# Routed rows kept as two 16-bit parts from PSUM on, transposed by DMA, and two tiles routed at once

## The chip, the cores and the metric

The kernel runs on one core of a Trainium2 chip. The metric is the device time of one execution in microseconds (us). Engines are named as in the profile: PE (TensorE matmul) and PEld (its weight loads), DVE (VectorE), ACT (ScalarE), POOL (GpSimd) and SP (SyncE, which issues nearly all DMAs here, in the order of its program).

## The reference

Local attention with ALiBi-like biases, then a dense layer of three maxed products, then a routed layer of eight experts, each token in its best one:

```python
x = attention(q, k, v)                                  # 3072 tokens x 512
h = np.maximum(np.maximum(x @ w1, x @ w2), x @ w3)      # 512 -> 768
x = h @ w_out                                           # 768 -> 512
logits = x @ w_gate
e_idx = np.argmax(logits, axis=1)
gate_w = softmax(logits)[np.arange(N), e_idx]
eom = 1.0 / (1.0 + np.exp(-(x @ w_output_gate)))
for e in range(8):
    mask = e_idx == e
    ye = np.maximum(x[mask] @ w1[e], 0.0) @ w2[e]       # 512 -> 1024 -> 512
    out[mask] = gate_w[mask, None] * eom[mask, e, None] * ye
```

All inputs are float32, and products are made from two 16-bit parts of each operand (high times high, high times low, low times high).

## The kernel before

The 3072 tokens are 24 tiles of 128 rows. Most of the program is written out by a planner: `Plan.run` picks from open tasks (generators that yield `op`, `dma`, `take` and `need`) the operation that by its own costs can start first, and so fixes the order on every engine. Engines then run their own list in order and wait at semaphores.

- **Attention** (tiles u = 0 to 23: `a_T`, `a_v`, `a_scores`, `a_trans`, `a_out`). `a_trans` transposes 512 KB of 16-bit weights by a DMA from SP (L1001).
- **Dense layer** in chunks of two tiles (`m_load`, `m_1`, `m_max`, `m_2`), woven into the attention from chunk 0 on. PE work of `m_1` is L1134, that of `m_2` is L1191.
- **Routing**, one task `m_route` per tile. `m_2` copies the second product out of PSUM as float32 rows `x2`. `split_T` transposes them on PE (L1065, four 128x128 float32 transposes), ACT copies the high part out and DVE makes the low part (`x2s`). Eight gate matmuls (L1225), a matmul that sums parts and turns the result (L1237), some 18 small DVE operations, two matmuls that count places (L1256, L1257), and POOL scatters the rows to `xs` in DRAM by expert (L1294).
- **First expert** (`pro_load`, `pro_1`, `pro_next`): the expert with most of the first 16 tiles' tokens is run on 256 rows while the last tiles are routed and `lists` works out the steps of the loop.
- **Expert loop** (`step`, 13 steps of two tiles here; `own` 0 and 1 are its two experts). PE order in a step: first product of own 0 (L1673, 96 matmuls), four float32 transposes of the next rows (`x_T`, L1595), first product of own 1, four transposes, second product of own 0, second product of own 1 (L1627). ACT and DVE split the transposed rows (L1597, L200). `load` fetches the rows for the step after that (L1586), and `split` takes the weights of the next expert, 8 pieces of 512 KB, from float32 to two parts and has each buffer loaded again (L1565).

L195 and L200 are the lines of the helpers `sub` and `low_of`, which many steps share.

Of the kernel before, what the change touches and what calls it, by code (L numbers as in the profile page):

```python
# [67 lines left out]
class Plan:  # L68
# [310 lines left out]
def local_attention_moe_kernel(  # L379
# [41 lines left out]
    make_identity(nc, ident)  # L421

# [131 lines left out]
    def buf(tag):  # L554
# [20 lines left out]
    wgp = cp.tile([P, KD, 4 * E], F32R, name="wgp")  # L575

    x_t = [mo.tile([P, D], F32, name=f"x{n}") for n in range(2)]
    x2_all = mo.tile([P, -(-3 * XW // LINE) * LINE], F32, name="x2r")
    x2_t = [x2_all[:, n * XW : (n + 1) * XW] for n in range(3)]
    stock("x", x_t)  # L580
    stock("x2s", [[mo.tile([P, KD, P], F32R, name=f"x2s{n}") for n in range(2)]])
# [8 lines left out]
                lg=mo.tile([4 * E, P], F32, name=f"lg{n}"),  # L590
                pz=mo.tile([P, 2 * E], F32, name=f"pz{n}"),
                rt=mo.tile([P, 5, E], F32, name=f"rt{n}"),
                rs=mo.tile([P, 6], F32, name=f"rs{n}"),
                ob=mo.tile([P, E], BF16, name=f"ob{n}"),
                di=mo.tile([P, 1], I32, name=f"di{n}"),
                one=mo.tile([P, 1], F32, name=f"one{n}"),
            )
            for n in range(2)
# [70 lines left out]
    def route_constants():  # L669
# [389 lines left out]
    def split_T(src, x, dst, s):  # L1059

        bank = yield take("bank")
        pt = bank.t.rearrange("p (a b) -> p a b", b=P)
        for d in range(KD):
            yield op(PE, 0.109, [src], [bank])
            nc.tensor.transpose(pt[:, d, :], x[:, d * P : (d + 1) * P], ident)  # L1065
        h, l = dst.t[0][:, :, s], dst.t[1][:, :, s]
        yield op(ACT, act(D), [bank], [dst])
        nc.scalar.copy(out=h, in_=pt)
        yield psum(dve(D), [bank, dst], [dst])
        sub(nc.vector, l, pt, h.bitcast(F32))  # L1070
        give("bank", bank)

# [105 lines left out]
    def m_2(c, t):  # L1178
# [29 lines left out]
        yield op(DVE, 0.2, [x2], [])  # L1208
        at = A_L + NTILE + tile_
        nc.vector.tensor_reduce(out=chk[:, at : at + 1], in_=x2.t[:, :NLOW], axis=AX.X, op=ALU.max)  # L1210
        plan.add(m_route(tile_, x2), (0, tile_))


    def m_route(tile_, x2):
        yield need(("wg",))
        xs_ = yield take("x2s")
        state("x2s", tile_)
        yield from split_T(x2, x2.t, xs_, slice(0, P))
        bank = yield take("bank")

        pl = bank.t[: 4 * E, :P]
        for n, d in [(4 * E, 0), *((2 * E, d) for d in range(KD)), *((4 * E, d) for d in range(1, KD))]:
            yield op(PE, 0.06, [xs_], [bank])
            X = xs_.t[0 if n == 4 * E else 1]
            nc.tensor.matmul(  # L1225
                pl[:n], lhsT=wgp[:, d, :n], rhs=X[:, d, :], start=(n, d) == (4 * E, 0), stop=(n, d) == (4 * E, KD - 1)
            )
# [3 lines left out]
        yield op(ACT, 0.25, [bank], [rb])  # L1231
        nc.scalar.copy(out=R["lg"], in_=pl)
        give("bank", bank)
        bank = yield take("bank")
        pz_ = bank.t[:, : 2 * E]
        yield op(PE, 0.19, [rb], [bank])
        nc.tensor.matmul(pz_, lhsT=R["lg"], rhs=two, start=True, stop=True)  # L1237
        pz, rt, rs, ob, di = R["pz"], R["rt"], R["rs"], R["ob"], R["di"]
        lz, tm, oh, ex, tz = [rt[:, n] for n in range(5)]
        mx, km, se, zs, co, de = [rs[:, n : n + 1] for n in range(6)]  # L1240
        yield psum(0.166, [bank], [rb])
        nc.vector.tensor_reduce(out=mx, in_=pz_[:, :E], axis=AX.X, op=ALU.max)

        yield psum(0.226, [bank, rb], [rb])
        nc.vector.scalar_tensor_tensor(out=tm, in0=pz_[:, :E], scalar=mx, in1=rev, op0=ALU.is_ge, op1=ALU.mult)
        yield op(DVE, 0.16, [rb], [rb])
        nc.vector.tensor_reduce(out=km, in_=tm, axis=AX.X, op=ALU.max)
        yield op(DVE, 0.18, [rb], [rb])
        nc.vector.tensor_scalar(out=ob, in0=rev, scalar1=km, scalar2=None, op0=ALU.is_equal)
        yield psum(0.18, [bank], [rb])  # L1250
        nc.vector.tensor_copy(out=pz, in_=pz_)
        give("bank", bank)
        bank = yield take("bank")
        pr = bank.t[:, : 2 * E].rearrange("p (a b) -> p a b", a=2)
        yield op(PE, 0.02, [rb], [bank])
        nc.tensor.matmul(pr[:, 0, :], lhsT=tri, rhs=ob, start=True, stop=True)  # L1256
        nc.tensor.matmul(pr[:, 1, :], lhsT=ones, rhs=ob, start=True, stop=True)  # L1257
        yield op(DVE, 0.16, [rb], [rb])
        nc.vector.tensor_scalar(out=lz, in0=pz[:, :E], scalar1=mx, scalar2=None, op0=ALU.subtract)
        yield op(DVE, 0.18, [], [])  # L1260
        nc.vector.tensor_scalar(out=oh, in0=rev, scalar1=km, scalar2=None, op0=ALU.is_equal)
        yield op(ACT, 0.4, [], [])
        nc.scalar.activation(out=ex, in_=lz, func=AF.Exp, accum_out=se)
        yield op(DVE, 0.16, [], [])
        nc.vector.tensor_mul(out=tz, in0=oh, in1=pz[:, E:])
        yield op(DVE, 0.16, [], [rb])
        nc.vector.tensor_reduce(out=zs, in_=tz, axis=AX.X, op=ALU.add)
        if tile_:
            yield need(("cnt", tile_ - 1), *([("snap",)] if tile_ == NFIRST else []))
        yield psum(0.16, [bank], [])  # L1270
        nc.vector.tensor_add(out=tm, in0=cnt, in1=pr[:, 0, :])
        yield op(DVE, 0.16, [], [])
        nc.vector.tensor_add(out=cnt, in0=cnt, in1=pr[:, 1, :])
        give("bank", bank)
        state("cnt", tile_)
        if tile_ == NFIRST - 1:
# [4 lines left out]
        nc.vector.tensor_tensor_reduce(out=tm, in0=tm, in1=oh, scale=1.0, scalar=0.0, op0=ALU.mult, op1=ALU.add, accum_out=de)  # L1281
        yield op(DVE, 0.16, [], [])
        nc.vector.tensor_copy(out=di, in_=de)
        yield op(ACT, 0.2, [rb], [rb])
        nc.scalar.activation(out=zs, in_=zs, func=AF.Exp, scale=-1.0)
# [4 lines left out]
        yield op(DVE, 0.16, [], [x2, rb])  # L1290
        nc.vector.reciprocal(out=x2.t[:, D + 1 :], in_=co)  # L1291
        yield op(POOL, 1.1, [x2, rb], [], 2.0, port=False)
        nc.gpsimd.memset(R["one"], 1.0)
        i = nc.gpsimd.indirect_dma_start(  # L1294
            out=xs[:, :], out_offset=bass.IndirectOffsetOnAxis(ap=di[:, 0:1], axis=0), in_=x2.t[:, :], in_offset=None
        )
        apart(i, "every token has a row of its own")
        give("x2r", x2)
        give("rt", rb)
        state("routed", tile_)  # L1300
# [270 lines left out]
    def fresh():  # L1571
# [3 lines left out]
        for name in ("pTx", "pg00", "pg01", "pg10", "pg11", "pc", "pd"):  # L1575
            T[name] = Buf(None, True)
# [11 lines left out]
    def x_T(half, step=False):  # L1588

        xr, xb = G["xr"][half], T[f"xT{half}"]  # L1590
        pTx = G["pTx"].rearrange("p (a b) -> p a b", b=P)
        xh, xl = [t[:, :, half * P : (half + 1) * P] for t in G["xE"]]
        for d in range(KD):
# [4 lines left out]
        yield psum(dve(D) + 0.07, [T["pTx"], xb], [xb])  # L1598
        low_of(nc, xl, pTx, XS, xh, G["sums"][:, NPC + half : NPC + half + 1] if step else G["acc"][:, NS + 6 + half : NS + 7 + half])
# [56 lines left out]
    def step(then, pl):  # L1656
# [5 lines left out]
        for own in range(2):  # L1662
            W, Wb = G["W"][1 - own], T["W"][1 - own]
            xT = [t[:, :, own * P : (own + 1) * P] for t in G["xE"]]
            for half in range(2):
# [11 lines left out]
                at = NPC + 2 + 2 * own + half  # L1677
# [6 lines left out]
            yield from x_T(own, True)  # L1684
# [12 lines left out]
    def pro_load():  # L1697
# [13 lines left out]
        G["xE"] = xT.t  # L1711
        for t, xb in enumerate(xbs):
            bank = yield take("bank")
            pt = bank.t.rearrange("p (a b) -> p a b", b=P)
            for d in range(KD):
                yield op(PE, 0.109, [xb], [bank])
                nc.tensor.transpose(pt[:, d, :], xb.t[:, d * P : (d + 1) * P], ident)
# [215 lines left out]
```

## Time and profile before

| | |
|---|---|
| time, median of 3 runs (lowest, highest) | 921.12 us (920.97, 921.45) |
| the profiled execution: time, span | 920.74 us, 919.2 us |
| PE busy | 851.1 us (93% of the span) |
| DVE, ACT, POOL busy | 689.0, 498.8, 225.2 us |
| DMA queue of SP, share of 16 engines' time | 56.2% |

The span is the stretch that the trace covers; the 1.5 us beside it lie before and after. The attention's last output is at about 471 us, the dense layer's last product ends at 592 us, and the loop runs from 617 to about 902 us. Busy time of PE counts each matmul until its modelled end, and neighbours overlap, so what an instruction costs on PE is read from the distance between starts.

### The profile page before, as it was taken

What the parts mean: (1) busy time and instruction counts of PE and PEld (TensorE: products, weight loads), DVE (VectorE), ACT (ScalarE), POOL (GpSimd) and SP (SyncE); (2) the same over time, 40 slices, a digit from 0 to 9 for tenths busy, and PEclk for the clock granted to TensorE, in tenths of its full rate; (3) what the DMA queues carried; (4) which work ended last, traced back from release to release, by engine and by line L of the source; (5) the groups of instructions that cost most, each with busy time, mean ns of one, the idle gap of its engine ahead of it and who ended that gap; (6) DMA issues with size and microseconds to landing.
All of it is one profiled execution on the core that took longest, in us unless ns stands there. A gap on an engine that the chain in (4) does not pass through costs nothing. (4 is left out here: it accounts for less than half of the span.)

```text
span 919.2 us, 24473 instructions
## 1 busy us (share of the span) xinstructions
PE 851.1 (93%) x8737; PEld 662.6 (72%) x8737; DVE 689.0 (75%) x2163; ACT 498.8 (54%) x1095; POOL 225.2 (24%) x245
## 2 busy tenths in 40 slices
PE   3566999899999999999999999999999999999993
PEld 2456876787878787878787787767777777777771
DVE  5998877888887877887767743367777777777774
ACT  4777766666666657576526322215555555555552
POOL 3444432223122213212101001012222222222222
PEclk9978999999999999999999999999999999999997
DMA  6997467777757776684558000047777766766600
GB/s 197 263 248 208 98 130 136 156 159 178 158 128 168 177 150 133 153 194 105 128 161 310 14 24 24 2 147 267 253 242 233 246 235 220 238 227 217 217 23 26
DMA packets 218907, 151.51 MB, mean 165 GB/s; under 512 B 181025, under 2 KB 181025, under 8 KB 218821
## 3 DMA queue, kind: packets, MB, share of 16 engines
q1 hardware_dynamic: 214658, 137.79, 56.2%
q0 software_dynamic: 4160, 12.62, 3.6%
q8 instruction: 48, 0.79, 0.4%
q14 instruction: 39, 0.31, 0.1%
q10 hardware_dynamic: 2, 0.00, 0.0%
HBM read 118.56 MB, written 23.11 MB: 154 GB/s over the span
## 5 line engine op out<-in xcount | busy, mean ns | idle before, releaser
L1134 PE MATMUL bank<-xT,w 128*128 128x256 f16 x2592 | 306.2, 275 | 2.7 <-ACT xT L1101 1.4
L1134 PEld LDWEIGHTS <-w 128*128 128x128 f16 x2592 | 249.3, 99 | 40.6 <-issue 6.6
L1673 PEld LDWEIGHTS <-we 128*128 128x128 f16 x2496 | 141.6, 98 | 4.6 <-ACTq L1877 0.8
L1673 PE MATMUL bank<-xT,we 128*128 128x128 f16 x2496 | 144.0, 219 | 0.9 <-DVEq L1877 0.6
L1627 PEld LDWEIGHTS <-he 128*128 128x128 f16 x672 | 65.7, 98 | 75.7
L981 ACT ACTIVATE sp<-sp,mn 128x232 f32<-128x232 f32 (+1 forms) x192 | 90.1, 470 | 45.1 <-DVE mn L974 43.9
L1616 ACT ACTIVATE hm<-bank 128x512 f32<-128x512 f32 x56 | 33.5, 597 | 136.8 <-issue 92.0
L1191 PE MATMUL bank<-w,hh 128*128 128x512 f16 x432 | 102.4, 379 | 0.0
L1156 DVE SCALAR_TENSOR_TENSOR hm<-bank,hm 128x512 f32<-128x512 f32 x72 | 49.7, 690 | 54.9 <-PE bank L1134 51.9
L1294 POOL DMA_INDIRECT xs<-x2r,di x24 | 24.6, 1026 | 238.3 <-DVE x2r L1291 99.8
L1627 PE MATMUL bank<-we,he 128*128 128x512 f16 x360 | 80.3, 379 | 0.0
L1627 PE MATMUL bank<-wp,he 128*128 128x512 f16 x312 | 69.5, 379 | 0.0
L1191 PEld LDWEIGHTS <-hh 128*128 128x128 f16 x432 | 40.7, 98 | 39.2 <-DVE hh L195 0.5
L200 DVE SCALAR_TENSOR_TENSOR wp<-ws,wp 128x1024 f16<-128x1024 f32 x56 | 66.2, 1217 | 0.0
L851 POOL TENSOR_SCALAR qkn<-qkn,vs 128x512 f32<-128x512 f32 x23 | 39.0, 1696 | 102.6 <-DVE vs L846 57.4
L974 DVE CUSTOM_DVE_ANT_0 sp<-bank,bias 128x232 f32<-128x232 f32 x160 | 60.1, 388 | 2.6 <-PE bank L950 2.5
L195 POOL TENSOR_TENSOR seen<-x,dco 128x1 f32<-128x1 f32 x14 | 13.2, 940 | 193.4 <-DVE x L1632 193.4
L200 DVE SCALAR_TENSOR_TENSOR we<-ws,we 128x1024 f16<-128x1024 f32 x49 | 59.7, 1220 | 0.0
L950 PE MATMUL bank<-k,qh 64*128 64x232 f32 (+1 forms) x384 | 44.0, 318 | 16.7 <-ACT k L924 12.0
L200 DVE SCALAR_TENSOR_TENSOR he<-hm,he 128x512 f16<-128x512 f32 x56 | 38.8, 692 | 20.2 <-ACT he L1620 17.0
L195 DVE TENSOR_TENSOR nat<-sp,nat 128x928 f16<-128x928 f32 (+1 forms) x46 | 52.7, 1146 | 1.3 <-ACT nat L995 0.3
L1549 ACT ACTIVATE wp<-ws 128x1024 f16<-128x1024 f32 x55 | 53.4, 1044 | 0.0
(264 smaller groups left out, 1402.4 us busy)
## 6 DMA issues: line engine op xcount, KB each, us to landing
ws<-in_moe_w_dram SPq DMA_DIRECT2D x112, 512.0 KB
raw<-in_moe_w_dram SPq DMA_DIRECT2D x12, 768.0 KB
bias<-in_moe_w_dram SPq DMA_DIRECT2D x16, 512.0 KB
x2r<-xs SPq DMA_DIRECT2D x30, 257.0 KB
qkn<-in_q_dram SPq DMA_DIRECT2D x23, 256.0 KB
qkn<-in_k_dram SPq DMA_DIRECT2D x23, 256.0 KB
qkn<-vd SPq DMA_DIRECT2D x23, 256.0 KB
qkn<-in_v_dram SPq DMA_DIRECT2D x23, 256.0 KB
```

What stands on the lines that cost most here:

```text
L195: eng.tensor_tensor(out=out, in0=in0, in1=in1, op=ALU.subtract)
L200: nc.vector.scalar_tensor_tensor(out=out, in0=x, scalar=scale, in1=high, op0=ALU.mult, op1=ALU.subtract, accum_out=total)
L851: nc.gpsimd.tensor_scalar(out=vf, in0=vf, scalar1=scale, scalar2=None, op0=ALU.mult)
L950: nc.tensor.matmul(sc[j][:, hp, :nw_], lhsT=x, rhs=y, start=(n < 2), stop=(n >= len(terms) - 2))
L974: nc.vector.tensor_tensor_reduce(out=o[:, g:], in0=x[:, g:], in1=bias[:, pr, n0 + g :], scale=scale, scalar=low, op0=ALU.add, op1=ALU.min, ...
L981: nc.scalar.activation(out=o, in_=o, func=AF.Exp, scale=-1.0, bias=mn[:, h : h + 1], accum_out=sm[:, h : h + 1])
L1134: nc.tensor.matmul(pj[:, f2, :], lhsT=w_at(j, part, d)[:, fs], rhs=X[:, d, :], start=(d + n == 0), stop=(d == KD - 1 and n == 2))
L1156: nc.vector.scalar_tensor_tensor(out=hv, in0=pj, scalar=1.0 / WS, in1=hv, op0=ALU.mult, op1=ALU.max)
L1191: nc.tensor.matmul(bank.t, lhsT=X[:, f, t * P : (t + 1) * P], rhs=w_at(3, part, f), start=(f + n == 0), stop=(f == KF - 1 and n == 2))
L1549: nc.scalar.mul(out=h, in_=s.t, mul=XS)
L1627: nc.tensor.matmul(py, lhsT=at(A_), rhs=w, start=(f + m == 0), stop=(last and m == 2))
L1673: nc.tensor.matmul(pg[:, f, :], lhsT=W[d][B_][:, fs], rhs=xT[A_][:, d, :], start=(d + m == 0), stop=(d == KD - 1 and m == 2))
```

## The change

- `m_2` writes the rows of the second product as a 16-bit high and a 16-bit low part side by side, in the 2048 bytes per row that the float32 row had (`parts`); ACT makes the high part and DVE the low one, both from PSUM. The scatter to `xs` moves the same bytes.
- `rows_T` transposes these 128x1024 16-bit rows. With `pe_` false one DMA from SP does it, straight into the operand; with `pe_` true PE does it in eight 16-bit transposes, and ACT and DVE copy the result. PE is used for the last chunk's two tiles and in `pro_next`; the DMA is used for the other 22 routed tiles, in `pro_load` and in every step of the loop.
- `m_route` handles both tiles of a chunk: eight gate matmuls of 256 columns in 16 bits in place of twice eight of 128 in float32r, two matmuls L1237 as before, five counting matmuls in place of twice two, and DVE operations on two tiles at a time.
- The split of the transposed rows by ACT and DVE goes (`split_T`, and in `x_T` and `pro_load`).

```diff
-    x2_all = mo.tile([P, -(-3 * XW // LINE) * LINE], F32, name="x2r")
-    x2_t = [x2_all[:, n * XW : (n + 1) * XW] for n in range(3)]
+    XB = -(-XW // LINE) * LINE
+    x2_all = mo.tile([P, 3 * XB], F32, name="x2r")
+    x2_t = [x2_all[:, n * XB : n * XB + XW] for n in range(3)]
-    stock("x2s", [[mo.tile([P, KD, P], F32R, name=f"x2s{n}") for n in range(2)]])
+    stock("x2s", [mo.tile([P, 2 * KD, 2 * P], F16, name="x2s")])
...
+        rows = parts(x2.t)
         yield op(ACT, act(D), [bank], [x2])
-        nc.scalar.mul(out=x2.t[:, :D], in_=bank.t, mul=1.0 / (XS * WS))
+        nc.scalar.mul(out=rows[:, :D], in_=bank.t, mul=1.0 / WS)
+        yield psum(dve(D) + 0.07, [bank, x2], [x2])
+        low_of(nc, rows[:, D:], bank.t, 1.0 / WS, rows[:, :D], chk[:, NTILE + tile_ : NTILE + tile_ + 1])
...
+        yield from rows_T(rows, x2, xs_.t, t, xs_, c == NCHUNK - 1, lambda: take("bank"))
...
+        if t:
+            plan.add(m_route(c, M["x2", c], xs_), (0, tile_))
+
+    def parts(rows):
+
+        return rows.bitcast(F16)[:, : 2 * D]
+
+    def rows_T(rows, src, dst, t, dstb, pe_, get=None):
+
+        at = dst[:, :, t * P : (t + 1) * P]
+        if not pe_:
+            yield dma(P * 2 * D * 2, [src], [dstb], rate=DMA_RATE_ROWS)
+            nc.sync.dma_start_transpose(out=at, in_=rows)
+            return
+        bank = yield get()
+        pt = bank.t.bitcast(F16).rearrange("p (a b) -> p a b", b=P)
+        for d in range(2 * KD):
+            yield op(PE, 0.06, [src], [bank])
+            nc.tensor.transpose(pt[:, d, :], rows[:, d * P : (d + 1) * P], ident16)
+        yield op(ACT, act(D), [bank], [dstb])
+        nc.scalar.copy(out=at[:, :KD], in_=pt[:, :KD])
+        yield psum(dve(D), [bank], [dstb])
+        nc.vector.tensor_copy(out=at[:, KD:], in_=pt[:, KD:])
+        give("bank", bank)
+
+    def m_route(c, x2, xs_):
...
-        yield from split_T(x2, x2.t, xs_, slice(0, P))
-        pl = bank.t[: 4 * E, :P]
+        pl = bank.t[: 4 * E, : 2 * P]
...
-            yield op(PE, 0.06, [xs_], [bank])
-            X = xs_.t[0 if n == 4 * E else 1]
+            yield op(PE, 0.112, [xs_], [bank])
+            X = xs_.t[:, d if n == 4 * E else KD + d, :]
...
+        for n, ws in enumerate(((tri,), (ones, tri), (ones, ones))):
+            for t, w in enumerate(ws):
+                nc.tensor.matmul(pr[:, n, :], lhsT=w, rhs=ob[:, t], start=(t == 0), stop=(t == len(ws) - 1))
...
-    def x_T(half, step=False):
+    def x_T(half, pe_=False):
-        for d in range(KD):
-            yield op(PE, 0.109, [T[f"xr{half}"]], [T["pTx"]])
-            nc.tensor.transpose(pTx[:, d, :], xr[:, d * P : (d + 1) * P], ident)
-        yield op(ACT, act(D), [T["pTx"]], [xb])
-        nc.scalar.mul(out=xh, in_=pTx, mul=XS)
+        yield from rows_T(parts(G["xr"][half]), T[f"xr{half}"], G["full"], half, T[f"xT{half}"], pe_, lambda: take("bank"))
...
-            yield from x_T(own, True)
+            yield from x_T(own)
...
+            yield from rows_T(parts(xb.t), xb, xT.full, t, xT, False)
```

What this moves is seen in the order of the instructions. On SP a step of the loop began with the load of the next rows of own 0 (`x2r<-xs`) and the weight pieces (`ws`); ISA rows are waits and register work:

```order
L1877 ISA
L1583 TENSOR_LOAD rowi
L1583 ISA x2
L1586 ISA
L1586 DMA x2r<-xs 128x514
L1560 ISA
L1560 TENSOR_LOAD esi
L1560 ISA x2
L1565 ISA
L1565 REGISTER_ALU
L1565 DMA ws_6895<-in_moe_w_dram 128x1024
```

After the change the step begins on SP like this:

```order
L1223 DMA_TRANSPOSE xT_745<-x2r 128x8x128
L1881 ISA
L1608 TENSOR_LOAD rowi
L1608 ISA x2
L1611 ISA x2
L1611 DMA x2r<-xs 128x514
L1585 ISA
L1585 TENSOR_LOAD esi
L1585 ISA x2
L1590 ISA
L1590 REGISTER_ALU
L1590 DMA ws_6443<-in_moe_w_dram 128x1024
```

A transpose now stands ahead of the load that overwrites its source, and so ahead of all weight pieces of the step. The second one stands behind the third weight piece:

```order
L1590 DMA bias<-in_moe_w_dram 128x1024
L1223 REGISTER_ALU
L1223 DMA_TRANSPOSE xT_745<-x2r 128x8x128
L1608 ISA
L1608 TENSOR_LOAD owni
L1608 ISA x2
L1611 ISA x2
L1611 DMA x2r<-xs 128x514
L1590 ISA x2
L1590 DMA ws_6437<-in_moe_w_dram 128x1024
```

Five weight pieces are left behind it; before, they stood behind two pieces and a load. On PE, in one of the late chunks, a routed tile was this between the dense layer's matmuls (gate matmuls, the turning one, the counting ones, and the next tile's transposes):

```order
L1225 MATMUL bank_526<-x2s_543,wgp 32x128
L1225 MATMUL bank_526<-x2s_544,wgp 16x128 x4
L1225 MATMUL bank_526<-x2s_543,wgp 32x128 x3
...
L1237 MATMUL bank_520<-two,lg_547 128x16
...
L1256 LDWEIGHTS tri
L1256 MATMUL bank_525<-ob_551,tri 128x8
L1257 LDWEIGHTS ones
L1257 MATMUL bank_525<-ob_551,ones 128x8
L1065 MATMUL bank_527<-ident,x2r 128x128 x4
```

After the change both tiles of a late chunk are this (of eight gate matmuls two are shown, of five counting ones two):

```order
L1244 MATMUL bank_524<-x2s,wgp 16x256
L1244 LDWEIGHTS wgp
L1244 MATMUL bank_524<-x2s,wgp 32x256
...
L1255 MATMUL bank_528<-two,lg_548 128x16 x2
...
L1284 LDWEIGHTS tri
L1284 MATMUL bank_529<-ob_551,tri 128x8
L1284 LDWEIGHTS ones
L1284 MATMUL bank_529<-ob_551,ones 128x8
```

The transposes are gone from PE, and the gate matmuls stand 48 matmuls of L1134's kind (256 columns) behind the last matmul of the chunk's second product in this chunk and in the next; in chunks 1 to 8 there is as much or more PE work between the two.

## Rows read from the trace of the kernel before

**Rows 1.** The page's 40 slices: PE's busy tenths and its granted clock.

```profile
PE   3566999899999999999999999999999999999993
PEclk9978999999999999999999999999999999999997
```

**Rows 2.** Windows: length, PE, PEld, DVE, ACT, POOL busy (count); clock, DMA share, GB/s.

```profile
100.00:200.00 100.00, 94.51 (x981) 75.02 (x981) 80.62 (x284) 64.56 (x171) 30.39 (x31) 0.98 0.64 130
200.00:300.00 100.00, 96.99 (x1035) 79.10 (x1036) 82.21 (x289) 62.84 (x171) 24.81 (x25) 1.00 0.72 160
300.00:604.00 304.00, 303.94 (x2939) 243.14 (x2938) 212.09 (x763) 150.28 (x386) 48.08 (x75) 1.00 0.47 120
640.00:860.00 220.00, 220.00 (x2489) 163.09 (x2487) 171.70 (x431) 115.60 (x150) 58.07 (x40) 1.00 0.71 235
```

**Rows 3.** Timeline of PE over one step of the loop: start, length, instructions.

```profile
705.79 5.52 PE L1673 MATMUL bank<-xT,we 128*128 128x128 f16 x96
711.15 0.61 PE L1595 MATMUL bank<-ident,x2r 128*128 128x128 f32 x4
711.59 5.52 PE L1673 MATMUL bank<-xT,we 128*128 128x128 f16 x96
716.95 0.61 PE L1595 MATMUL bank<-ident,x2r 128*128 128x128 f32 x4
717.39 5.34 PE L1627 MATMUL bank<-wp,he 128*128 128x512 f16 x24
727.75 5.52 PE L1673 MATMUL bank<-xT,we 128*128 128x128 f16 x96
```

**Rows 4.** Timeline of PE over one routed tile, late in the dense layer.

```profile
520.05 0.60 PE L1065 MATMUL bank<-ident,x2r 128*128 128x128 f32 x4
520.49 2.11 PE L1191 MATMUL bank<-w,hh 128*128 128x512 f16 x9
522.24 0.83 PE L1225 MATMUL bank<-x2s,wgp 128*32 128x128 f32 x8
522.91 0.82 PE L1191 MATMUL bank<-w,hh 128*128 128x512 f16 x3
523.67 0.39 PE L1237 MATMUL bank<-two,lg 32*128 32x16 f32 x2
523.99 1.48 PE L1134 MATMUL bank<-xT,w 128*128 128x256 f16 x12
525.31 0.17 PE L1256 MATMUL bank<-ob,tri 128*128 128x8 bf16 x1
525.36 0.64 PE L1065 MATMUL bank<-ident,x2r 128*128 128x128 f32 x4
```

**Rows 5.** Timeline of PE: a run of 256-column matmuls, and a transposed tile of `pro_load`.

```profile
531.39 16.54 PE L1134 MATMUL bank<-xT,w 128*128 128x256 f16 x150
547.76 0.60 PE L1717 MATMUL bank<-ident,x 128*128 128x128 f32 x4
548.20 1.46 PE L1191 MATMUL bank<-w,hh 128*128 128x512 f16 x6
```

**Rows 6.** SP's timeline: the attention's last DMA transpose (512 KB).

```profile
464.44 2.11 SPq L1001 DMA_TRANSPOSE aT<-nat  x1
```

**Rows 7.** Windows around that transpose, columns as in rows 2.

```profile
464.40:465.65 1.25, 1.25 (x14) 1.12 (x13) 1.01 (x10) 0.20 (x1) 0.00 (x0) 1.00 0.00 1
465.65:468.15 2.50, 2.50 (x43) 2.32 (x41) 1.24 (x5) 0.00 (x0) 0.96 (x1) 1.00 1.09 207
```

**Rows 8.** Waits of SP's queue over the whole span: total, times, longest.

```profile
SPq L1001 <- DVE nat L195: 65.4, 17, 13.6
```

**Rows 9.** Timelines of ACT and DVE: a tile's rows leaving PSUM, and the low part.

```profile
592.41 0.60 ACT L1202 ACTIVATE x2r<-bank 128x512 f32<-128x512 f32 x1 [0.41 <-PE bank L1191]
714.13 0.69 DVE L200 SCALAR_TENSOR_TENSOR xT<-bank,xT 128x512 f16<-128x512 f32 x1
714.75 0.08 DVE L200 DVE_READ_ACCUMULATOR xT<-bank,xT 128x1 f32 x1
```

**Rows 10.** Timeline of SP over the loads of one step (L1586 rows, L1565 weights).

```profile
703.04 6.48 SPq L1565 DMA_DIRECT2D ws<-in_moe_w_dram  x5
714.40 0.35 SPq L1586 DMA_DIRECT2D x2r<-xs  x1
```

More of the change, by code (lines that the diff above doesn't have):

```diff
@@ L589, in local_attention_moe_kernel @@
             dict(
[L590 to L596, printed above, removed]
+                lg=mo.tile([4 * E, 2 * P], F32, name=f"lg{n}"),
+                rt=mo.tile([P, 4, 2, E], F32, name=f"rt{n}"),
+                rs=mo.tile([P, 8, 2], F32, name=f"rs{n}"),
+                ob=mo.tile([P, 2, 2 * E], BF16, name=f"ob{n}"),
+                di=mo.tile([P, 16], I32, name=f"di{n}"),
+                one=mo.tile([P, 16], F32, name=f"one{n}"),
             )
-            for n in range(2)
+            for n in range(1)
         ],
@@ L1207, in m_2 @@
         )
[L1208 to L1214, printed above, removed]
+        if t == 0:
+            M["x2s", c], M["x2", c] = (yield take("x2s")), []
+            state("x2s", c)
+        yield need(("x2s", c))
+        xs_ = M["x2s", c]
+        M["x2", c].append(x2)
+        yield from rows_T(rows, x2, xs_.t, t, xs_, c == NCHUNK - 1, lambda: take("bank"))
@@ L1230, in m_route @@
         R = rb.t
-        yield op(ACT, 0.25, [bank], [rb])
-        nc.scalar.copy(out=R["lg"], in_=pl)
+        yield op(ACT, 0.39, [bank], [rb])
+        nc.scalar.mul(out=R["lg"], in_=pl, mul=1.0 / (XS * WS))
         give("bank", bank)
         bank = yield take("bank")
[L1235 to L1238, printed above, removed]
@@ L1248, in m_route @@
[L1248 to L1251, printed above, removed]
+        pz = bank.t[:, : 4 * E].rearrange("p (t e) -> p t e", t=2)
+        for t in range(2):
+            yield op(PE, 0.19, [rb], [bank])
+            nc.tensor.matmul(pz[:, t], lhsT=R["lg"][:, t * P : (t + 1) * P], rhs=two, start=True, stop=True)
+        lz, tm, ex, tz = [R["rt"][:, n] for n in range(4)]
@@ new lines, in m_route, with each @@
+        ob, di = R["ob"][:, :, :E], R["di"][:, :2]
+        mx, km, se, zs, co = [R["rs"][:, n] for n in range(5)]
+        def each(x):
+            return x.unsqueeze(2).to_broadcast([P, 2, E])
+        both = rev.unsqueeze(1).to_broadcast([P, 2, E])
+        yield psum(0.18, [bank], [rb])
+        nc.vector.tensor_reduce(out=mx, in_=pz[:, :, :E], axis=AX.X, op=ALU.max)
+        yield psum(0.2, [bank, rb], [rb])
+        sub(nc.vector, lz, pz[:, :, :E], each(mx))
+        yield op(DVE, 0.2, [rb], [rb])
@@ new lines, in m_route @@
+        nc.vector.scalar_tensor_tensor(out=tm, in0=lz, scalar=0.0, in1=both, op0=ALU.is_ge, op1=ALU.mult)
+        yield op(DVE, 0.18, [rb], [rb])
+        nc.vector.tensor_reduce(out=km, in_=tm, axis=AX.X, op=ALU.max)
+        yield op(DVE, 0.2, [rb], [rb])
+        nc.vector.tensor_tensor(out=ob, in0=both, in1=each(km), op=ALU.is_equal)
+        yield op(ACT, 0.2, [rb], [])
+        nc.scalar.activation(out=ex, in_=lz, func=AF.Exp)
+        yield psum(0.2, [bank, rb], [rb])
+        nc.vector.tensor_mul(out=tz, in0=ob, in1=pz[:, :, E:])
@@ new lines, in m_route @@
+        yield op(DVE, 0.18, [], [rb])
+        nc.vector.tensor_reduce(out=zs, in_=tz, axis=AX.X, op=ALU.add)
+        yield op(ACT, 0.2, [rb], [rb])
+        nc.scalar.activation(out=zs, in_=zs, func=AF.Exp, scale=-1.0)
+        if c:
+            yield need(("cnt", 2 * c - 1), *([("snap",)] if 2 * c == NFIRST else []))
+        yield psum(0.2, [bank], [])
+        nc.vector.tensor_add(out=tm, in0=pr[:, 0:2], in1=cnt.unsqueeze(1).to_broadcast([P, 2, E]))
+        yield op(DVE, 0.16, [], [])
+        nc.vector.tensor_add(out=cnt, in0=cnt, in1=pr[:, 2])
@@ L1274, in m_route @@
         give("bank", bank)
-        state("cnt", tile_)
-        if tile_ == NFIRST - 1:
+        for t in range(2):
+            state("cnt", 2 * c + t)
+        if 2 * c + 2 == NFIRST:
             yield op(DVE, 0.16)
@@ L1280, in m_route @@
         yield op(DVE, 0.2, [], [])
[L1281 to L1285, printed above, removed]
+        nc.vector.tensor_mul(out=tm, in0=tm, in1=ob)
+        yield op(DVE, 0.18, [], [])
+        with nc.allow_low_precision(reason="one whole number among zeros"):
+            nc.vector.tensor_reduce(out=di, in_=tm, axis=AX.X, op=ALU.add)
+        yield op(DVE, 0.18, [rb], [])
+        nc.vector.tensor_reduce(out=se, in_=ex, axis=AX.X, op=ALU.add)
         yield op(DVE, 0.16, [], [])
@@ L1289, in m_route @@
         nc.vector.scalar_tensor_tensor(out=co, in0=zs, scalar=1.0, in1=se, op0=ALU.add, op1=ALU.mult)
[L1290 to L1298, printed above, removed]
+        for t in range(2):
+            yield op(DVE, 0.16, [], [x2[t], rb])
+            nc.vector.reciprocal(out=x2[t].t[:, D + 1 :], in_=co[:, t : t + 1])
+        for t in range(2):
+            yield op(POOL, 1.1, [x2[t], rb], [], 2.0, port=False)
+            nc.gpsimd.memset(R["one"][:, t : t + 1], 1.0)
+            i = nc.gpsimd.indirect_dma_start(
+                out=xs[:, :], out_offset=bass.IndirectOffsetOnAxis(ap=di[:, t : t + 1], axis=0), in_=x2[t].t[:, :], in_offset=None
+            )
+            apart(i, "every token has a row of its own")
+            give("x2r", x2[t])
+            state("routed", 2 * c + t)
         give("rt", rb)
-        state("routed", tile_)
     NL = MAXT - 2
@@ L1676, in step @@
                 places = [t[:, 4 * half : 4 * half + 4, own * P : (own + 1) * P] for t in G["hE"]]
-                at = NPC + 2 + 2 * own + half
+                at = NPC + 2 * own + half
                 r = T[f"r{half}"]
@@ L1710, in pro_load @@
         T["xT"] = xT = yield take("xT")
-        G["xE"] = xT.t
+        G["xE"], G["full"] = xT.t, xT.full
         for t, xb in enumerate(xbs):
[L1713 to L1717, printed above, removed]
-            h, l = [x[:, :, t * P : (t + 1) * P] for x in G["xE"]]
-            yield op(ACT, act(D), [bank], [xT])
-            nc.scalar.mul(out=h, in_=pt, mul=XS)
-            yield psum(dve(D) + 0.07, [bank, xT], [xT])
-            low_of(nc, l, pt, XS, h, G["acc"][:, NS + 4 + t : NS + 5 + t])
-            give("bank", bank)
+            yield from rows_T(parts(xb.t), xb, xT.full, t, xT, False)
             give("x", xb)
```

88 lines of the change are left out of this document (24 added, 64 removed).

## Prediction

> **What bounds the kernel now.** I read the page's slices first. PE's busy tenths stand at 9 in every slice from the fifth on but one (an 8) and the last, and its granted clock at 9 there but for the last [rows 1]. The windows then tell how full that is: 94.5 and 97.0 of 100 us in the second and third hundred, 303.9 of 304 us from 300 on, and all of 220 us inside the expert loop, while DVE, the next one, has 0.70 to 0.82 in each [rows 2]. In the trace a step of the loop is a chain of PE work with nothing between: it starts at 705.79 and the next at 727.75, so 21.96 us, and the four pieces shown meet without a gap [rows 3]. So from about 100 us on the time is the sum of what PE is given to do; what leaves PE leaves the time, and what is added elsewhere costs only where PE comes to wait for it. Both the removed and the added work lie behind 100 us, since the first tile is routed there.
>
> **What PE loses in the loop.** Twice a step PE transposes 128 rows in float32. The mean duration of these matmuls hides their cost because they overlap; the distance between starts shows it: 711.15 to 711.59, and 716.95 to 717.39, so 0.44 us for four [rows 3]. That is 0.88 us a step, and 13 steps give **11.4 us**. Nothing is added to PE in the loop.
>
> **What PE loses in routing.** A tile takes, from start to start: transposes 0.44, gate matmuls 0.67, the turning matmul 0.32, the two counting ones 0.05, in all 1.48 us [rows 4]; a pair 2.96. After the change a pair has eight gate matmuls of 256 columns in 16 bits. No row shows these, but the dense layer's have the same shape of moving operand: 150 in 16.37 us, so 0.109 each [rows 5] and 0.87 for eight. The lower bound is the 0.67 of one tile's eight, the upper twice that, 1.34 [rows 4]; I take 0.87, as the data type is that of the dense row. With two turning matmuls (0.64) and five counting ones at 0.025 (0.13) the pair is 1.64 us, 1.32 less. Eleven pairs give **14.5 us** (12.0 at 1.87 for the eight gates' upper bound, 16.7 at the lower). The last pair still has 16 PE transposes, now of 16-bit data; 96 matmuls of 128 columns in 16 bits take 5.36 us, 0.056 each [rows 3], so 0.89 for 16, and the pair saves only **0.4**. `pro_load` loses two transposed tiles at 547.76 to 548.20 each, 0.44 [rows 5], **0.9**. `pro_next` swaps four transposes of 0.44 for eight of 0.45: nothing.
>
> **What is added off PE.** 22 + 2 + 26 DMA transposes of 256 KB. The trace of before has transposes of 512 KB. The last one is alone on the queues: issued at 464.44 [rows 6], the DMA engines start about 1.2 us later and are done at about 468.15, after 2.5 us at 207 GB/s [rows 7] (a scatter joins them at the end). For half the bytes the lower bound is 1.2 + 1.25 = 2.45 us from issue to landing and the upper that of the whole, 3.7. I take 2.5, as the time follows the bytes once the engines run, plus what is queued ahead. In the loop the result is wanted much later: own 0's transpose may start when its first product ends (5.4 us into the step) and must be there at the next step's start, after own 1's first product and both second products, 5.4 + 10.3 = 15.7 us; own 1's has as long. In routing it is covered by the dense matmuls put ahead of the gate matmuls: in the late chunks 48 of 0.109, 5.2 us from the last product's end. ACT's eviction (0.60) and DVE's low part with its read (0.77) come first [rows 9], so 3.8 us are left for 2.5 to 3.7. That is tight only at the upper bound; without that cover each of 11 pairs would cost up to 3.7 us.
>
> Here the Trainium skill has a rule against the change. "VectorE: DVE Perf Modes", section "The three transpose paths", gives 390 ns for a 128x128 16-bit transpose on TensorE and 1309 ns for one by DMA, and its rules for authors say to take TensorE where a PSUM destination will do. By 1309 ns for each of the eight blocks of a row tile a transpose would be 10.5 us, an estimate from that page. The trace doesn't agree for transposes of many blocks: 16 blocks take 2.5 us of engine time, 0.16 each [rows 7].
>
> DMA time: a step has 0.71 of 21.96, 15.6 us [rows 2]; two transposes of 1.25 add 2.5 to 2.7 (their share reads 1.09), so 18.2 of a new step of 21.1. Full, but not the bound. SP: the transpose of own 0 stands ahead of the reload of its source, which must wait for it, and of the weight pieces; so SP is held for 2.5 to 3.7 us, twice a step. Before, SP had issued a step's loads by 709.5 and then nothing until 714.40 [rows 10], so the first hold falls into that pause. The second delays five weight pieces by some 3 us; each is used a step after it is issued, so nothing on PE is late.
>
> ACT loses a pass of 512 columns for each tile in routing and loop, and DVE a low part in the loop and half of the small operations of routing. I count this as nothing: PE covers it, and as it is a loss of work, no cover can go.
>
> **Sum.** 11.4 + 14.5 + 0.4 + 0.9 = 27.2 us. The profiled execution took 920.74, 0.04% below the median of 921.12; 920.74 - 27.2 = **893.5 us**, about 3% faster. What a measurement of this kernel can tell from no change is about 0.2%, 1.8 us.
>
> **The rivals.**
> - *The attention stage keeps its time.* The planner makes a new order for every engine from the first routed tile on, and PE is not quite full from 100 to 300 us [rows 2]. If DVE, ACT or a DMA sets the pace there, the eight pairs routed before 470 us give nothing: 8 x 1.32 = 10.6, time 904.1. Against it: PE has no idle time worth naming from 300 on, and DVE, at 0.8, loses work. Chance 0.11.
> - *PE's idle time goes too.* The 8.5 us that PE stood idle from 100 to 300 us [rows 2] are partly waits for DVE and ACT, which lose work: up to 8.5 more, 885.0. The planner's order is not made for that. Chance 0.06.
> - *The loop becomes bound by DMA.* While SP is held, only what it has issued runs. If the engines ran dry through both holds of 3.7 us, a step would need 15.6 + 7.4 = 23.0 us, 1.0 more than now: 13.5 lost in place of 11.4 won, time 918.4. Halfway, at 22 us, it is 905. It takes both holds dry, and there are weight pieces in flight ahead of the second. Chance 0.04.
> - *Slower: gate matmuls wait behind the attention's transposes.* SP issues in order, and it waited 65.4 us, once 13.6, for DVE before its transposes [rows 8]. A routing transpose behind such a one lands late, and PE, which is in order too, stops at the gate matmul with all dense work behind it. It decides from 27.2 / 11 = 2.5 us a pair: at 2.8 us the time is 924.3. Against it: those waits are mostly SP with nothing else to do, and in the chunks of the attention the gates stand 5 to 17 us of PE work behind the second product. Chance 0.03.
> - *Each block is transposed for itself.* If the start-up of 1.25 us were paid for each of eight blocks of 0.16, a transpose would hold the queue 11.3 us; a step of the loop would be 15.6 + 22.6 = 38.2 us, and 13 of them would add 211 us: 920.7 - 15.8 + 211 = 1116. The Trainium skill's page "VectorE: DVE Perf Modes" (section above) bears on this case. The 2.5 us of 16 blocks [rows 7] speak against it. Chance 0.01.
>
> **How the numbers follow.** The forecast has the remaining 0.75; its own range is 889 to 899, by the bounds of the gate matmuls (2.5 either way) and as much again for the new order. The range of 885 to 904.5 takes in the first two rivals, 0.92 by these cases, and I go no wider, as the rest lies far off. Faster by over 0.2%: 0.75 + 0.11 + 0.06 + 0.03 (most of the DMA case) = 0.95; within 0.2%: 0.01; slower: 0.04.
>
> **What the profile after would show.** The loop's step is 21.08 us from start to start of own 0's first product, with the 96 matmuls of own 1 directly behind the 96 of own 0; the loop's DMA share is 0.83 to 0.87. PE from 300 us to the loop is full, without an idle time before the gate matmuls named after a DMA. A late pair is 1.64 us of PE. The loop starts about 15.8 us earlier, at 601 to 602. I am wrong if PE waits for the transposed rows at a gate matmul or at a step's start, if the step stays near 22 us, or if PE's idle time between 100 and 300 us grows by more than a few us.

## The result, and the profile after

The changed kernel takes **910.1 us** (median of 4 runs, 908.23 to 913.39) against 921.29 (4 runs, 920.97 to 922.18): ratio 0.9881, 95% interval 0.9847 to 0.9914. It is 1.2% faster, where 3% was forecast; the time lies above the range. The profiled execution took 908.63 us, with a span of 907.1.

From the page of the changed kernel: the busy time of the engines, PE's slices as in [rows 1], and of the costliest groups one (busy time, mean of one, idle time before them and what ended most of it):

```profile
PE 829.1 (91%) x8469; PEld 638.4 (70%) x8469; DVE 641.0 (71%) x1911; ACT 473.7 (52%) x994; POOL 197.8 (22%) x245
...
PE   3566799999999999999999999979999999989993
...
L1689 PE MATMUL bank<-xT,we 128*128 128x128 f16 x2496 | 145.8, 222 | 13.2 <-DMA xT<-x2r 7.4
```

PE lost 22 us of busy time, but three of its slices read less than before: the 5th, early in the attention (over the first 200 us PE is as busy as before, 152.7 us against 151.9), the 27th, which is the entry of the loop, and the 36th, late in it. The last row is the loop's first products (L1689, L1673 before): PE now stands 13.2 us ahead of them, 7.4 of that for transposed rows and 5.8 at the loop's entry.

Windows of the changed kernel, with the columns of [rows 2]:

```profile
100.00:200.00 100.00, 94.06 (x997) 74.81 (x996) 81.74 (x264) 62.54 (x163) 28.91 (x30) 0.98 0.71 152
200.00:300.00 100.00, 98.59 (x1030) 77.76 (x1028) 80.89 (x271) 64.17 (x171) 29.31 (x31) 1.00 0.82 179
300.00:588.00 288.00, 286.11 (x2734) 225.60 (x2733) 181.92 (x595) 129.11 (x307) 42.09 (x68) 1.00 0.55 133
640.00:860.00 220.00, 212.57 (x2391) 155.12 (x2389) 154.07 (x380) 113.23 (x140) 40.12 (x40) 0.99 0.82 247
```

Ahead of the loop PE is about as full as before: it gains 1.6 us from 200 to 300 us and loses 1.8 behind 300. In the loop it is not full: 212.57 of 220 us. PE's timeline at the loop's entry, over the step in which it first waits, and over that of the longest wait:

```profile
600.53 0.61 PE L1229 MATMUL bank<-ident,x2r 128*128 128x128 f16 x8
606.91 12.71 PE L1689 MATMUL bank<-xT,we 128*128 128x128 f16 x192 [5.77 <-SPq L1881]
619.45 5.34 PE L1643 MATMUL bank<-wp,he 128*128 128x512 f16 x24
...
629.81 10.88 PE L1689 MATMUL bank<-xT,we 128*128 128x128 f16 x192
...
650.89 10.88 PE L1689 MATMUL bank<-xT,we 128*128 128x128 f16 x192
...
735.21 5.52 PE L1689 MATMUL bank<-xT,we 128*128 128x128 f16 x96
742.00 5.53 PE L1689 MATMUL bank<-xT,we 128*128 128x128 f16 x96 [1.27 <-DMA xT<-x2r]
...
802.75 5.52 PE L1689 MATMUL bank<-xT,we 128*128 128x128 f16 x96
810.76 7.16 PE L1689 MATMUL bank<-xT,we 128*128 128x128 f16 x96 [2.49 <-DMA xT<-x2r]
817.76 5.34 PE L1643 MATMUL bank<-wp,he 128*128 128x512 f16 x24
```

PE is done with the work ahead of the loop at 601.1 (616.6 before) and then stands for 5.77 us until SP enters the loop (L1881). The step from 629.81 to 650.89 is 21.08 us, own 1's 96 matmuls directly behind own 0's. At 735.21 they come 6.79 us behind, not 5.36.

The whole account, from the two traces: the work ahead of the loop ends 15.4 us earlier; the gap at the entry grows from 0.3 to 5.8, so 5.5 are given back; the 13 steps, from the first matmul to the last product's end, take 285.9 us (606.91 to 892.85) in place of 286.8 (616.86 to 903.65; the loop of before ends there, not at about 902), so 0.9 won; the end behind the loop is 1.3 shorter. 15.4 - 5.5 + 0.9 + 1.3 = 12.1, the difference of the spans.

**Why the entry waits.** SP's timeline before it enters the loop (L1611 loads rows; L1551 stages weight pieces, four of which are in rows left out here):

```profile
595.97 2.12 SPq L1611 DMA_DIRECT2D x2r<-xs  x2
...
601.94 0.33 SPq L1611 DMA_DIRECT2D x2r<-xs  x1
602.46 0.97 SPq L1551 DMA_DIRECT2D ws<-in_moe_w_dram  x2
604.28 0.34 SPq L1611 DMA_DIRECT2D x2r<-xs  x1
604.82 0.99 SPq L1551 DMA_DIRECT2D ws<-in_moe_w_dram  x2
```

Between the lists and the loop SP issues four row loads and eight weight pieces, until 605.8. Before the change nothing in the loop that PE's first matmul reads was written by SP: `xT` came from ACT and DVE. Now `xT` is written by SP's DMA inside the loop, and PE's first matmul waits until SP is there. The clock falls meanwhile (windows of the changed kernel):

```profile
602.00:604.00 2.00, 0.00 (x0) 0.00 (x0) 0.45 (x3) 0.00 (x0) 0.48 (x1) 0.99 1.04 414
604.00:606.00 2.00, 0.00 (x0) 0.00 (x0) 0.00 (x1) 0.00 (x0) 0.53 (x1) 0.50 1.03 414
...
608.00:610.00 2.00, 2.00 (x22) 2.00 (x20) 0.00 (x0) 0.00 (x0) 0.00 (x0) 0.50 1.04 409
610.00:612.00 2.00, 2.00 (x32) 2.00 (x30) 0.00 (x0) 0.20 (x1) 0.00 (x0) 0.81 1.06 405
```

PE has stood since 601.1; the granted clock is 0.50 (1.2 GHz) from 604 to 610, and the first products take 12.54 us (606.91 to 619.45) in place of 10.72: 1.8 more.

**Why the later steps wait.** SP's timeline of one step of the loop, and its waits from 630 to 860 us (total, times, longest):

```profile
659.73 1.27 SPq L1223 DMA_TRANSPOSE xT<-x2r  x1
664.63 0.37 SPq L1611 DMA_DIRECT2D x2r<-xs  x1
666.24 1.18 SPq L1590 DMA_DIRECT2D ws<-in_moe_w_dram  x2
667.90 0.33 SPq L1590 DMA_DIRECT2D bias<-in_moe_w_dram  x1
668.55 1.28 SPq L1223 DMA_TRANSPOSE xT<-x2r  x1
674.64 0.35 SPq L1611 DMA_DIRECT2D x2r<-xs  x1
675.55 3.99 SPq L1590 DMA_DIRECT2D ws<-in_moe_w_dram  x5
681.95 1.27 SPq L1223 DMA_TRANSPOSE xT<-x2r  x1
```
```profile
SPq L1611 <- DMA xT<-x2r: 56.9, 20, 4.1
```

The load that overwrites a transpose's source is issued only when the transpose has landed, and stands right behind it on SP. Own 0's holds SP from 659.73 to 664.63, 4.9 us; own 1's, behind three weight pieces, from 668.55 to 674.64, 6.1 us. A third hold stands at the turn of the loop: SP has issued its last weight piece by 656.9 and PE is done with own 0's product at 656.25, but the transpose goes out at 659.73. A semaphore that it waits for has its last count from a weight piece issued at 653.48, which lands at 659.58; in ten more steps too the transpose goes out right behind such a landing, and SP stands for 1.0 to 2.2 us before it. So it is not PE that SP waits for there. SP's own step is 22.2 us here, from 659.73 to 681.95; the transposes of own 1 were issued at 645.80 and, four steps later, at 735.80, 22.5 us apart. PE's step is 21.08, so each step takes 1.4 us of the lead. The one issued at 645.80 had landed by 651.76, 4.5 us early for its matmul (650.89 + 5.36 = 656.25); four steps on they are late. From 735 on, PE's first products of own 1 start late in five steps: 6.79, 6.97, 6.57, 8.01 and 6.68 us behind those of own 0 in place of 5.36, 8.2 us together. Behind the longest wait the granted clock is 0.69 and 0.74 (811 to 817), and own 1's products take 7.00 us (810.76 to 817.76) in place of 5.37: 9.9 us in all.

### The profile page after: what moved, and what is told of

Its sections match the earlier page's. It is cut to its first block, busy times and chain, and to the rows that moved or that the text cites. A ratio compares the mean times of both kernels' runs of the same rounds, so it can differ in the third digit from the quotient of the medians.

```text
span 907.1 us, 23690 instructions
## 1 busy us (share of the span) xinstructions
PE 829.1 (91%) x8469; PEld 638.4 (70%) x8469; DVE 641.0 (71%) x1911; ACT 473.7 (52%) x994; POOL 197.8 (22%) x245
## 5 line engine op out<-in xcount | busy, mean ns | idle before, releaser
L1689 PE MATMUL bank<-xT,we 128*128 128x128 f16 x2496 | 145.8, 222 | 13.2 <-DMA xT<-x2r 7.4
L1689 PEld LDWEIGHTS <-we 128*128 128x128 f16 x2496 | 143.8, 99 | 17.0 <-DMA xT<-x2r 8.3
L195 POOL TENSOR_TENSOR seen<-x,dco 128x1 f32<-128x1 f32 x14 | 13.2, 940 | 208.6 <-DVE x L1648 208.6
L1636 DVE CAST he<-hm 128x512 f16<-128x512 f32 x29 | 12.4, 427 | 62.7 <-ACT hm L1632 62.6
```

What stands on the lines that cost most here:

```text
L195: eng.tensor_tensor(out=out, in0=in0, in1=in1, op=ALU.subtract)
L1689: nc.tensor.matmul(pg[:, f, :], lhsT=W[d][B_][:, fs], rhs=xT[A_][:, d, :], start=(d + m == 0), stop=(d == KD - 1 and m == 2))
```

## The experiments

Two theories stood after these readings. By the first (A in the expectations), both losses are matters of SP's order: SP comes late into the loop, and in each step it stands at the reload until a transpose has landed. The main rival (C) has the DMA engines themselves as the limit of the loop, at a share of 0.82 with all waits counted; then another order on SP would not help.

**e1_pe_loop: transposes of the loop on PE, in 16 bits.**

```diff
-            yield from x_T(own)
+            yield from x_T_pe(own)
```

`x_T_pe` is `rows_T` with `pe_` true and a bank that is kept.

> The changed kernel, but the loop's rows are transposed by PE in 16 bits (eight transposes, ACT and DVE copy), as the start of the loop has it; routing as changed. Theory A (routing gave its 15.6 us; in the loop the DMA transposes lose more than they give, at the entry because PE waits until SP has entered the loop, and later because SP is held between a transpose and the reload of its source): no wait of PE at the entry over 1 us, every step 21.9 to 22.0 us, no wait for transposed rows, time 904 to 906. Rival B (the entry wait is for data, rows or weights that land late, whoever transposes): the 5.8 us at the entry stay, time 911 to 913.

Measured: 907.36 us (905.63 to 908.52), ratio 0.9853 (0.9837 to 0.9870). PE's waits from 595 to 880 us are only these, and its work ahead of the loop ends with the row behind them:

```profile
PE bank L1701 <- DVE xT L1233: 1.4, 1, 1.4
PE bank L1623 <- DMA x2r<-xs: 1.1, 1, 1.1
```
```profile
602.68 0.61 PE L1229 MATMUL bank<-ident,x2r 128*128 128x128 f16 x8
```

Without SP's DMA as the writer of `xT`, the wait of 5.8 us and the late rows are both gone, although every step pays its two transposes again: 22.0 us, as before the change. Entry wait and time are a little above what was expected; PE's work ahead of the loop, the same in both kernels, ended at 603.3, 2.2 later than in the changed kernel. (In the changed kernel and the six variants that leave this work as it is, but for the engine that issues its last loads, it ended between 599.9 and 603.3: one trace tells it no better than that.) So in the kernel as changed, the loop's DMA transposes bring nothing over transposes of the same 16-bit rows on PE.

**e2_late: the reload of the rows behind the second product.** Everything else of the loop, its bytes too, stays.

```diff
             yield from x_T(own)
-            yield from load(("rowi", "owni")[own], then, own)
...
                     pl.state("second", own, f // 2)
+            yield from load(("rowi", "owni")[own], then, own)
```

> The changed kernel with one thing moved: the reload of the rows is issued behind the second products' matmuls, so that no weight piece stands behind it; same DMA transposes, same bytes. Theory A (SP's own chain sets 22.5 us a step: each transpose's landing time of 5 to 6 us is waited out by SP before it issues anything else): steps of 21.1 us throughout, no wait for transposed rows, the entry wait of 5.8 us stays, time 898 to 900. Rival C (the DMA engines' time sets the 22.5 us): steps grow to over 22 us late in the loop as before, time 907 to 911.

Measured: 899.63 us (898.67 to 902.11), ratio 0.9782 (0.9763 to 0.9802). Its window of the loop, and SP's timeline from own 1's transpose on:

```profile
640.00:860.00 220.00, 220.00 (x2473) 159.44 (x2471) 162.26 (x400) 120.31 (x150) 41.00 (x41) 1.00 0.85 259
```
```profile
666.22 1.40 SPq L1223 DMA_TRANSPOSE xT<-x2r  x1
668.20 0.34 SPq L1590 DMA_DIRECT2D ws<-in_moe_w_dram  x1
670.47 0.34 SPq L1611 DMA_DIRECT2D x2r<-xs  x1
```

SP goes on to a weight piece 2.0 us after the transpose, PE is full and all steps are 21.08 us. The DMA engines carry 259 GB/s at a share of 0.85, more than the 247 at 0.82 of the changed kernel: they were not its limit, and the rival falls. The entry keeps its wait (5.6 us) and its slow clock: the first products take 13.4 us.

**e7_less: three weight pieces fewer in the loop.**

```diff
-            yield dma(P * FE * 4, w=[s])
-            nc.sync.dma_start(out=view(s.t), in_=src, cond=G["more"], cond_hint=True)
+            if d >= 3:
+                yield dma(P * FE * 4, w=[s])
+                nc.sync.dma_start(out=view(s.t), in_=src, cond=G["more"], cond_hint=True)
```

> The changed kernel, but in the loop the first three of the eight weight pieces aren't loaded again (those parts of later experts' weights stay those of an earlier one); it leaves out 1.5 MB a step that stand on SP's queue ahead of the second transpose. Theory A (that transpose lands 6 us after its issue because it queues behind those pieces): it lands in 3 to 4 us, no late waits, steps of 21.1 us, time 896 to 900. Rival (the transposes themselves take 5 to 6 us in the loop): second transpose still lands after 5 us or more.

Measured: 897.92 us in one run; the entry keeps its wait, 5.7 us. SP's timeline, with the order of the changed kernel otherwise:

```profile
657.59 1.26 SPq L1223 DMA_TRANSPOSE xT<-x2r  x1
660.82 0.36 SPq L1612 DMA_DIRECT2D x2r<-xs  x1
662.55 1.29 SPq L1223 DMA_TRANSPOSE xT<-x2r  x1
665.76 0.36 SPq L1612 DMA_DIRECT2D x2r<-xs  x1
```

Both transposes land after 3.2 us, and no rows are late. Nothing is in flight ahead of them here: the three pieces ahead of own 1's are taken out, and the five ahead of own 0's have landed, as SP had issued them some 5 us before (the DMA share is 0.06 from 657 to 658 us). So what made 4.9 and 6.1 us of 3.2 was the weight pieces in flight, and the rival falls. The changed kernel agrees: behind the last three transposes of its loop, issued at 871.39, 878.51 and 885.28, when weights are no longer loaded, SP goes on after 3.2 us each.

**e4_pool_entry: SP's issues before the loop given to POOL.** The eight weight pieces and the last two row loads; the loop stays as changed.

```diff
-            nc.sync.dma_start(out=view(s.t), in_=src)
+            (nc.sync if e < 2 else nc.gpsimd).dma_start(out=view(s.t), in_=src)
...
-            yield from load(("rowi", "owni")[own], bass.ds(1, 1), own)
+            nc.gpsimd.dma_start(out=G["xr"][own], in_=xs[bass.ds(r, P), :])
```

> The changed kernel, but the ten transfers that SP issues between the lists and the loop (eight weight pieces, two row tiles for the second step) are issued by POOL, so SP reaches the loop earlier; the loop is as changed. Theory A (PE's first matmul waits for SP to enter the loop): the entry wait falls from 5.8 us to under 2, PE's clock does not fall there, the late waits in the loop stay, time 901 to 903. Rival B (the wait is for data): the wait stays 5 us or more, as the same bytes land no earlier; time 908 or more.

Measured: 907.62 us (904.96 to 909.74), ratio 0.9870 (0.9851 to 0.9889). PE's waits from 595 to 880 us, but for two of 0.2:

```profile
PE bank L1692 <- DMA xT<-x2r: 10.3, 9, 2.5
PE bank L1692 <- ACTq L1887: 1.3, 1, 1.3
```

The entry's wait went as expected, and the first products take 10.88 us (602.75 to 613.63), so the clock stays. The time was missed: the late rows grew from five waits of 7.4 us to nine of 10.3. With PE kept at the entry, SP had started the loop with a lead; without that, PE comes to wait some four steps earlier. The first loss had hidden a part of the second.

**e4_late_pool: both mends.** The edits of e2_late and e4_pool_entry together.

> Both mends at once: the reload of the rows behind the second products, and the ten transfers ahead of the loop issued by POOL. Theory A (the two losses are apart and add up): entry wait under 2 us with the clock kept, 13 steps of 21.1 us without a wait for transposed rows, 892 to 895 us. Rival (with SP no longer late at the entry, the DMA engines' 0.85 share now makes PE wait somewhere else in the loop): 897 us or more.

Measured: **891.98 us** (890.74 to 895.40, 5 runs), ratio 0.9704 (0.9684 to 0.9723). PE's timeline at the entry, and the window of the loop:

```profile
601.70 11.07 PE L1692 MATMUL bank<-xT,we 128*128 128x128 f16 x192 [1.76 <-ACTq L1887]
...
622.97 10.88 PE L1692 MATMUL bank<-xT,we 128*128 128x128 f16 x192
...
644.04 10.88 PE L1692 MATMUL bank<-xT,we 128*128 128x128 f16 x192
```
```profile
640.00:860.00 220.00, 220.00 (x2513) 161.08 (x2512) 160.34 (x394) 112.93 (x142) 44.21 (x44) 1.00 0.83 254
```

The loop starts at 601.7, its steps are 21.1 us and PE is full. This version is faster than both kernels, and its time is near that of the forecast.

**e4_late_pool_ws: the same, but the row loads stay with SP.**

> As e4_late_pool, but the two row tiles for the second step stay with SP; POOL issues the eight weight pieces alone. The second of those loads waits until PE has transposed and ACT and DVE have copied the first step's rows, so SP enters the loop some 2 to 3 us after PE is done. Theory A (PE waits for SP's entry, however little SP has to issue): entry wait of 2 to 4 us named after SP, 895 to 898 us. Rival (only the amount of SP's work before the loop counts): entry wait as in e4_late_pool, under 2 us, 892 to 895 us.

Measured: 893.30 us (891.21 to 896.06), ratio 0.9713 (0.9687 to 0.9738). The wait at the entry is named after SP again but small (`SPq L1884`, 1.9 us): wait and time came out as the rival there expected, so it is the amount of SP's work, mostly the weight pieces, that had kept SP out of the loop. Against e4_late_pool the intervals overlap, so the row loads' own share stays open.

**e5_pe_route: the routed tiles transposed on PE**, the loop as changed.

```diff
-        yield from rows_T(rows, x2, xs_.t, t, xs_, c == NCHUNK - 1, lambda: take("bank"))
+        yield from rows_T(rows, x2, xs_.t, t, xs_, True, lambda: take("bank"))
```

> The changed kernel with all 24 routed tiles transposed by PE in 16 bits (eight transposes, copies by ACT and DVE), in place of the last two alone; loop as changed. If the forecast's routing term is right (DMA transposes there cost PE nothing): 22 x 0.45 = 9.8 us more of PE ahead of the loop, which starts at about 616.5 in place of 606.9, time 917 to 919. If the DMA transposes made PE wait or slowed the attention: less than half of it, time under 914.

Measured: 915.52 us (912.99 to 925.48, 10 runs), ratio 0.9956 (0.9929 to 0.9984). PE's last work ahead of the loop, and the loop's start:

```profile
610.34 0.61 PE L1229 MATMUL bank<-ident,x2r 128*128 128x128 f16 x8
616.53 12.60 PE L1689 MATMUL bank<-xT,we 128*128 128x128 f16 x192 [5.58 <-SPq L1881]
```

The loss at the entry is the same. In these two traces the work ahead of the loop ends 9.8 us later than in the changed kernel (610.34 against 600.53), which would be the whole of 22 transposes of 0.45 us. But the time missed what was expected, 917 to 919, from below, and the profiled execution, 918.73, is one of the slow ones of the ten. By the medians the kernel is 5.4 us slower than the changed one, by the ratios to the kernel before 6.9. So the price on PE is shown in the main, and its full size is not.

**e6_pe_all: both on PE**, e1_pe_loop and e5_pe_route together; what is left is the pairing and the 16-bit gate matmuls.

> The changed kernel without any DMA transpose but the attention's: all routed tiles and all steps of the loop transposed by PE in 16 bits. What is left of the change is the pairing, the 16-bit gate matmuls and the 16-bit rows. By the forecast's terms: 12 pairs that save 2.96 - 1.64 - 0.90 = 0.42 us each, 5.0, and pro_load 0.9; loop as before; time 914 to 916. Rival (the pairing itself shortens or lengthens the attention stage by other waits): outside 911 to 919.

Measured: 915.14 us (913.38 to 918.46, 6 runs), ratio 0.9950 (0.9928 to 0.9972), as expected. Unlike what its text says, the two transposes of `pro_load` still go by DMA (0.9 us by the forecast). So pairing, 16 bits and these two are worth some 5 us, the other DMA transposes the rest of what e4_late_pool shows. PE's work ahead of the loop ends here:

```profile
606.87 0.61 PE L1229 MATMUL bank<-ident,x2r 128*128 128x128 f16 x8
```

That is 3.5 us before e5_pe_route with the same work, 6.3 behind the changed kernel and 4.2 behind e1_pe_loop. From e1_pe_loop to this run only the routing's transposes differ: 7.8 us by the medians, 8.9 by the ratios. All pairs together put what the routing's DMA transposes save at 4 to 10 us, where PE's price is 9.9. A small part of what is given back is seen: from 300 to 400 us PE is busy for 98.1 to 98.4 us in the seven kernels that transpose the routed tiles by DMA (in the changed one it waits 1.9 us for ACT, L842) and for 100.0 in these two. What gives back the rest stays open.

## Why the prediction failed

- **PE's work is the time:** right. With PE full (e4_late_pool) the time is 892.0, and the sum of what leaves PE had given 893.5. That it is so near is in part luck: in the trace the work ahead of the loop ends 16.6 us earlier than before (15.8 forecast) and the loop is 12.4 shorter (11.4), and of what was not foreseen the end behind the loop is 2.4 shorter and the entry 1.5 longer.
- **Routing, 15.8 us with the last pair and `pro_load`:** right as far as the traces tell; 15.4 us were measured, in an execution where this may be off by 1 or 2 (see e1_pe_loop), and by e5 and e6 the transposes' share may be smaller than forecast. The last pair after the change, without its transposes, on PE's timeline, against [rows 4]:

```profile
581.18 1.05 PE L1244 MATMUL bank<-x2s,wgp 128*32 128x256 f16 x8
582.16 0.50 PE L1668 MATMUL bank<-xT,we 128*128 128x256 f16 x3
582.69 0.61 PE L1255 MATMUL bank<-two,lg 32*128 32x16 f32 x4
583.24 1.16 PE L1668 MATMUL bank<-xT,we 128*128 128x256 f16 x9
584.40 0.17 PE L1284 MATMUL bank<-ob,tri 128*128 128x8 bf16 x1
```

  The eight gate matmuls take 0.98 us (0.87 forecast), the turning ones 0.55 (0.64), the counting ones 0.13 (the next products start at 584.53): 1.66 a pair against 1.64. The prediction's lower bound for the term, 12.0, is worked out wrongly: with 1.34 for the eight gates a pair is 2.11, which gives 9.4, so its own range of 889 to 899 was too narrow on the slow side. As the gates took 0.98, nothing hangs on it. No transpose is waited for by PE ahead of the loop, so the rival of waiting gate matmuls falls, and so does that of the attention stage, with PE as full from 100 to 300 us as before.
- **The loop's step of 21.08 us:** right, where the rows are there in time.
- **The landing, "2.5, as the time follows the bytes once the engines run, plus what is queued ahead":** the landing alone is 3.2 us (e7_less), inside the bounds. The error is that no number was put on what is queued ahead: with it the landing takes 4.9 and 6.1 us.
- **"So SP is held for 2.5 to 3.7 us, twice a step ... so nothing on PE is late":** this is the step that failed. The transposed rows are what is late, and what delays them is the hold of the step before. SP's own step with both holds was never added up against PE's: 22.5 against 21.08 us. The argument looked at one transpose, which has 15.7 us, and not at a chain that loses 1.4 us with each step. It cost 9.9 us. The third hold, at the turn of the loop, was not in the sum at all.
- **The loop's entry** was put at nothing without a reason: the prediction looked at SP's order inside a step, but not at SP's way into the loop. With `xT` filled by SP's DMA, PE waited there for SP: 5.8 us, and 1.8 for the clock.
- **The rivals:** "The loop becomes bound by DMA", at 0.04, had the place and, with 22 to 23 us, the size of the late steps; its chance was far too small, and the engines were not what was short. The loop can run its bytes in 21.08 us (e2_late).
- **DMA share 0.83 to 0.87:** right for a loop that runs at its pace (0.85 in e2_late, 0.83 in e4_late_pool), 0.82 with the waits.
- Not foreseen: the end behind the loop is 1.3 us shorter. Why is open.

Put together: 893.5 + 0.4 (15.4 for 15.8) + 5.5 and 1.8 at the entry + 9.9 of late rows - 1.3 at the end - 1.3 that the loop of before had lost at its own start (286.8 against 13 x 21.96) = 908.5, and the profiled execution took 908.63.

The rule of the Trainium skill's page "VectorE: DVE Perf Modes", section "Rules for kernel authors", to take TensorE, would have been as good for this loop as it stood: 907.4 us in e1_pe_loop. The price of a DMA transpose in the Trainium skill's page "VectorE: DVE Perf Modes", section "The three transpose paths", doesn't explain that: the 10.5 us estimated from it for eight blocks are 3.2 here, and with SP's order mended the DMA wins (892.0).

## What to carry to other kernels

Where a step of a loop moves to a queue that issues in order, add up that queue's own time for one step, with every hold behind a landing and what is queued ahead of it, and compare it with the step of the engine that sets the pace; being early once is not enough. Put what must wait for a landing (here the reload of the source) as late as it may stand. When a buffer gets a new writer inside a loop, look at what the writer still has to do before the loop, since the first reader may wait for it there, and expect one loss to hide a part of another.

## What the runs showed of the hardware

- A 256 KB transpose by DMA lands 3.2 us after its issue with nothing ahead (e7_less), and 4.9 to 7.4 us behind weight loads in the changed kernel's loop, read from the issue of the load that waits for it. It takes 1.27 us on the issuing queue, against 0.33 to 0.37 for a plain load.
- PE's granted clock was 0.50 from 604 us on, after PE had stood since 601.1, and was whole again in the window from 612 on. In e2_late PE stood from 601.9 to 607.5, and the clock still read 1.00 from 604 to 606 and 0.58 from 606 to 608. With 1.76 us of standing in e4_late_pool no fall is seen: the first products took 10.91 us (601.70 to 612.61).
- Executions spread by some 3 to 5 us in most variants, with late rows (908.2 to 913.4 us after the change) and without (890.7 to 895.4 in e4_late_pool), and by 12.5 in ten runs of e5_pe_route, against 918.8 to 922.7 in eleven of the kernel before. What makes the spread is open.
